# Order of ScalarE's and VectorE's copies around two transposes, and the place of one unit's loads, in an attention kernel with a gated feed-forward layer

## The chip, the cores and the metric

The kernel runs on one core of one Trainium2 chip. The metric is the device time of the whole program in microseconds (us), taken as the median over several runs. The engines are TensorE (PE, with PEld its weight loads), VectorE (DVE), ScalarE (ACT), GpSimd (POOL) and SyncE (SP, which here issues every DMA).

## The reference

Shapes: q, k, v are (4, 8, 576, 64), the feed-forward weights (512, 2048) and (2048, 512), all float32.

```python
scores = scale * np.matmul(q, k.transpose(0, 1, 3, 2))
x = (psi_rel / psi_i)[..., None]            # a position feature of each (i, j)
bias = np.maximum(x @ w1 + b1, 0.0) @ w2    # one value per (i, j) and head
scores = scores + bias.transpose(2, 0, 1)[None]
attn = np.exp(scores - np.max(scores, axis=-1, keepdims=True))
attn = attn / (np.sum(attn, axis=-1, keepdims=True) + 1e-09)
o = np.matmul(attn, v)                      # (B, H, S, D), then (B * S, H * D)
h = o @ w_in
out = (h * np.cos(h)) @ w_out
```

## The kernel before, in words

The program has three stages, and every order in it is written out by hand: each engine takes its instructions in the order in which the code names them.

**Bias stage.** A loop over n = 0 to 36 makes the 36 groups of bias rows. For each, VectorE (line 309) and for some ScalarE (line 311) make four tiles `ht`, TensorE multiplies them (line 325), ScalarE turns the product into `rt` (line 344; the group with index 34 is done by VectorE, line 342), and SP stores `rt` in a scratch tensor `sc` in DRAM (line 345). There are five `rt` buffers, so a sixth `rt` waits until the first one's store has landed. `load_bias` (line 234) reads whole bias tiles `bt` back. Between the groups stand the loads of q and k of the first units, and the transposes of unit 0's k and q.

**Attention stage.** A unit is a pair of heads of one batch entry: 16 units, numbered from 0. Each has five slots, j = 0 to 4, one for each tile of 128 query rows (`tiles = [0, 1, 4, 2, 3]`, where tile 4 holds the last 64 rows of both heads). `slot` writes, for each: the products `s` of q and k (line 413) and VectorE's pass over each head, which adds the bias and takes the minimum of the negated scores (line 426); the exponentials `P` of the slot before (`softmax_exp`, line 446, one call per head); transposes of the normalised `P` of three slots before (line 476), copied out of the PSUM tile `pm` half by ScalarE and half by VectorE (`keep_main`, lines 501 and 504); products with v (`pv`, line 542).

The next but one unit's q and k are also turned here, in two pieces. The left-overs (rows 512 to 575 of k and q, loaded into one tile) are turned in slot 1 into the PSUM tile `pt` (line 196), and `keep_turned(u, "x", ...)` copies k's part twice into `kt` on VectorE (line 211) and q's part twice into `qt` on ScalarE (line 214). The main pieces of q and k are turned in slot 2 into one PSUM tile `spare` (line 476), and `keep_pair` copies q on ScalarE (line 206) and k on VectorE (line 204). The framework lets two engines read one PSUM tile only one after the other, in the order of the code: the engine named second waits for the one named first. `spare` is one of two buffers with the tag `s`, so slot 3's second product needs it free again. For unit 0 all of this stands in slot 2.

`two` is true in slot 2 of units 0 to 13, the slots that turn a main piece.

**Feed-forward stage.** 96 steps of two matrix products each (lines 695 and 750), with the cosine gate between them.

Of the kernel before, what the change touches and what calls it, by code (L numbers as in the profile page):

```python
# [28 lines left out]
def kernel(  # L29
# [11 lines left out]
    nc = tc.nc  # L41
# [71 lines left out]
    with tc.manual_schedule():  # L113
# [19 lines left out]
        kt = st.tile([128, 640], F32, name="kt")  # L133
# [5 lines left out]
        def turned(u, x):  # L139
            return kt if x == "k" else qts[u % 2]  # L140
# [46 lines left out]
        def bank(dt=F32):  # L187
            return ps_t.tile([128, 512], dt, tag="t", name="pt")

        def natural(u, x):  # L190
            return nat[u, "k" if x == "x" else x].rearrange("p r h d -> p r (h d)")

        def turn(u, x, ps):
            n = natural(u, x)
            for i, c in enumerate((4,) if x == "x" else range(4)):
                nc.tensor.transpose(ps[:, 128 * i : 128 * i + 128], n[:, c], ident)
            return ps
# [9 lines left out]

        def keep_turned(u, x, ps):
            if x == "x":
                for at in (0, 576):  # L210
                    nc.vector.tensor_copy(kt[:, at : at + 64], ps[:, 0:64])
                for h in range(2):
                    r = slice(64 * h, 64 * h + 64)
                    nc.scalar.activation(  # L214
                        out=qts[u % 2][r, 512 + 64 * h : 576 + 64 * h], in_=ps[r, 64:128], func=AF.Copy, scale=-0.125
                    )
                return
            o = turned(u, x)[:, 64:576] if x == "k" else turned(u, x)[:, 0:512]
            nc.scalar.activation(
                out=o.rearrange("p (x c) -> p x c", c=4),  # L220
                in_=ps.rearrange("p (c x) -> p x c", c=4),
                func=AF.Copy,
                scale=-0.125 if x == "q" else 1.0,
            )
# [134 lines left out]
        for n in range(len(todo) + 1):  # L359
            now = hts  # L360
            if n < len(todo):
                hts = bias_hid(n + 1) if n + 1 < len(todo) else None
                ps = bias_rows(n, now)
            if held:
                bias_store(*held)
            for t in {19: (0,), 27: (1,), 36: (2, 3)}.get(n, ()):
                load_bias(0, t)
            if n == 11:
                load_bias(0, 4)
            held = (n, ps)  # L370
            if n == 6:
                for x in "kq":
                    load(1, x)
            if n == 16:
                for x in "kq":
                    load(2, x)
            if n in T_FIRST:
                keep_turned(*T_FIRST[n], turn(*T_FIRST[n], bank()))
            if n in S_FIRST:
                for step in S_FIRST[n][1]:  # L380
                    split(0, S_FIRST[n][0], step)
            if n == len(todo):
                abs_w(*wparts[0])
# [58 lines left out]
        def softmax_exp(u, j, h):  # L442
            neg, m = cur.pop((u, j, h))
            if h == 0:
                dn[u, j] = sv.tile([128, 2], F32, tag="dn", name="dn")
            nc.scalar.activation(  # L446
                out=P[u, j][:, 576 * h : 576 * h + 576],
                in_=neg,
                func=AF.Exp,
                bias=m[:, 0:1],  # L450
                scale=-1.0,
                accum_out=dn[u, j][:, h : h + 1],
            )
# [17 lines left out]
        def heads_of(x):  # L471
            return range(2 if tiles[x[1]] < 4 else 1)
# [99 lines left out]
        def slot(i):  # L572
            u, j = divmod(i, 5)
            now, last, prev = get(i), get(i - 1), get(i - 3)
            if now:
                spare = qk(u, j)
            two = now and j == 2 and u + 2 < NU
            for h in heads_of(last) if last else ():
                if h == 1 and two:
                    break  # L580
                softmax_exp(*last, h)
            if prev and prev[1] in (0, 2):
                alloc_half(prev[0], prev[1] // 2)
            first, ahead, behind = [[], []], [], []
            if two:
                for n, x in enumerate("qk"):
                    for c in range(4):
                        at = 256 * n + 64 * c
                        for r in range(2):
                            first[r].append((spare[:, r, at : at + 64], natural(u + 2, x)[:, c]))  # L590
            if prev and j in (2, 4):
                pair_ = [(u - 1, 3), (u - 1, 4)] if j == 2 else [(u, 0), (u, 1)]
                if pair_[0] in P:
                    src = [P[x][:, 512:640] for x in pair_]
                    shared[0] = bank(), src, (pair_[0][0], 0 if j == 4 else 1)
                if pair_[0] in P and (now or j == 4):
                    ahead = [(shared[0][0][:, 128 * n : 128 * n + 64], x) for n, x in enumerate(src)]
            elif j in (0, 3) and shared:
                gone = shared.pop(0)
                behind = [(gone[0][:, 128 * n + 64 : 128 * n + 128], x) for n, x in enumerate(gone[1])]  # L600
            pm = halves(prev, first, ahead, behind)
            if shared and not now and j == 2:
                gone = shared.pop(0)
                for n, x in enumerate(gone[1]):
                    nc.tensor.transpose(gone[0][:, 128 * n : 128 * n + 128], x, ident)
                behind = [gone]
            xt = None
            if i == 0:
                for x in "kq":
                    keep_turned(1, x, turn(1, x, ps_m.tile([128, 512], F32, tag="m0" if x == "k" else "m1", name="pm")))  # L610
                keep_turned(1, "x", turn(1, "x", bank()))
            if now and (j == 1 or i == 2) and i != 1 and u + 2 < NU:
                xt = turn(u + 2, "x", bank())
            for du, hf, chunks in PV_EARLY[j]:
                if 0 <= u + du < NU:
                    pv(u + du, hf, chunks)
            if two:
                keep_pair(u + 2, "q", spare[:, :, 0:256])
                keep_pair(u + 2, "k", spare[:, :, 256:512])
                softmax_exp(*last, 1)  # L620
            if prev:
                keep_main(*prev, 0, pm[0])
            for du, hf, chunks in PV_EARLY[j]:
                if 0 <= u + du < NU and 4 in chunks:
                    keep_x(u + du, hf)
            if prev:
                keep_main(*prev, 1, pm[1])
            if behind:
                keep_left(*gone[2], gone[0][:, 0:256])
            if last:  # L630
                recip(*last, 0)
                recip(*last, 1)
            if now and u == 0 and j == 0:
                split(1, "k")
            elif now and u == 0 and j == 1:
                split(1, "q")
            elif now:
                for du, x, step in POOL_PLAN[j]:
                    if u + du < NU and not (u == 0 and x == "q"):
                        split(u + du, x, step)  # L640
            if xt is not None:
                keep_turned(u + 2, "x", xt)
            if last:
                for h in heads_of(last):
                    norm(*last, h)
            if now:
                if i == 1:
                    load(0, "v")
                for du, x in LOAD_PLAN[j]:
                    if u + du < NU:  # L650
                        load(u + du, x)
                hp, b = units[u]
                if b == B - 1 and hp + 1 < HP:
                    load_bias(hp + 1, tiles[j])
                if u == NU - 1 and j < KD:
                    split_x(0, 0, j)
            for step, at in W_PLAN:
                w, r = divmod(i - 0 - at, 10)
                if r == 0 and 0 <= w < len(wparts):
                    if step == "load":  # L660
                        if w + 2 < len(wparts):
                            load_w(*wparts[w + 2])
                    elif step == "abs":
                        abs_w(*wparts[w])
                    else:
                        widen_w(*wparts[w], step)

        for i in range(len(jobs)):
            slot(i)
# [225 lines left out]
```

## Time and profile before

| | us or share |
|---|---|
| median of 3 runs | 731.68 (731.63 to 733.46) |
| the profiled execution's own time | 731.56 |
| its span | 729.8 |
| PE busy | 96% |
| DVE busy | 82% |
| ACT busy | 60% |
| POOL busy | 55% |

The span is the profiled part of the program, from its first to its last instruction; the execution's own time has a little more around it. A busy share is that of the whole span, over all three stages.

### The profile page before, as it was taken

The numbers are of one execution on the slowest core, as the hardware profiler recorded it, in microseconds if no ns is written. First come the engines' busy times: TensorE is split into PE (matmuls) and PEld (weight loads), VectorE is DVE, ScalarE is ACT, GpSimd is POOL, SyncE is SP. The second block draws the span as 40 slices with busy tenths as digits, with TensorE's granted clock in tenths as the row PEclk, the third lists the DMA queues.
The fourth block names the chain that finished last, engine by engine and source line by source line (L and its number), as shares of the span: only waits on it lengthen the run. The fifth ranks groups of instructions, "written<-read, shape, count | busy, mean of one in ns | idle before, by whom it ended". The sixth has DMA issues, their size and how long they took to land.

```text
span 729.8 us, 16094 instructions
## 1 busy us (share of the span) xinstructions
PE 701.4 (96%) x5960; PEld 569.9 (78%) x5960; DVE 600.5 (82%) x1371; ACT 435.7 (60%) x917; POOL 402.9 (55%) x486
## 2 busy tenths in 40 slices
PE   6888999999999999999999999999999999999997
PEld 4556766666666666768988989988989988989986
DVE  8988888888888888856778789898998999966665
ACT  6778777777867778754565555445454454443342
POOL 0203877877787787774456274564544463663300
PEclk9999999999999999999999999999999999999999
DMA  6688337434623730100011010102011110011112
GB/s 201 215 268 275 72 94 188 120 81 105 171 51 91 198 82 19 47 30 30 29 35 53 29 59 30 58 29 58 31 31 56 30 58 30 1 41 46 45 44 86
DMA packets 84398, 58.66 MB, mean 80 GB/s; under 512 B 62304, under 2 KB 70624, under 8 KB 84320
## 3 DMA queue, kind: packets, MB, share of 16 engines
q1 hardware_dynamic: 84320, 57.63, 27.6%
q8 instruction: 47, 0.77, 0.4%
q14 instruction: 31, 0.25, 0.1%
HBM read 42.00 MB, written 15.61 MB: 79 GB/s over the span
## 4 chain that ended last, share of the span: by engine, by line
PE 84%; DVE 8%; ACT 4%; DMA 2%; issue 2%; POOL 1%; SPq 0%; DVEq 0%; ACTq 0%; POOLq 0%
PE ph L695 28%; PE po L750 27%; PE pv L542 10%; PE s L413 9%; PE pa L325 4%; PE pm L476 4%; DVE P L426 3%; ACT P L446 2%; DVE ht L309 1%; DVE kt L204 1%; DMA sc<-rt 1%; ACT qt L206 1%; DVE PT L504 1%; ACT qt L214 1%; PE pt L476 1%
## 5 line engine op out<-in xcount | busy, mean ns | idle before, releaser
L469 POOL TENSOR_SCALAR P<-P,rc 128x576 f32<-128x576 f32 x144 | 108.2, 763 | 46.0 <-PE s L413 29.0
L426 DVE CUSTOM_DVE_ANT_0 P<-s,bt 128x576 f32<-128x576 f32 x144 | 103.8, 754 | 15.8 <-PE s L413 13.0
L699 ACT ACTIVATE a<-ph,quarter 128x384 int32<-128x384 f32 x96 | 55.7, 581 | 101.2 <-PE ph L695 100.1
L527 POOL TENSOR_TENSOR xs<-xT,xs 128x384 fp32r<-128x384 f32 x96 | 107.1, 1116 | 8.0
L446 ACT ACTIVATE P<-P,m 128x576 f32<-128x576 f32 x144 | 110.3, 769 | 0.7 <-DVE m L426 0.3
L413 PEld LDWEIGHTS s<-kN,qT 64*128 64x128 f32 (+1 forms) x864 | 72.2, 187 | 47.7 <-DVE m L426 14.8
L695 PE MATMUL ph<-xs,wpre 128*128 128x384 f32 x576 | 109.4, 338 | 0.0
L695 PE MATMUL ph<-xs,w 128*128 128x384 f32 x576 | 108.3, 337 | 0.0
L705 DVE SCALAR_TENSOR_TENSOR r<-a,ph 128x384 f32<-128x384 int32 x96 | 52.8, 550 | 67.0 <-ACT a L699 66.8
L695 PEld LDWEIGHTS ph<-xs,wpre 128*128 128x128 f32 x576 | 101.8, 188 | 5.7 <-DVE a L714 0.9
L413 PE MATMUL s<-kN,qT 64*128 64x288 f32 (+1 forms) x864 | 94.7, 314 | 11.9 <-DVE kt L204 10.0
L695 PEld LDWEIGHTS ph<-xs,w 128*128 128x128 f32 x576 | 101.5, 188 | 4.8 <-DVE a L714 0.6
L710 ACT ACTIVATE r<-r,hpi 128x384 f32<-128x384 f32 x96 | 59.3, 617 | 73.8 <-DVE r L706 73.6
L526 POOL TENSOR_SCALAR xs<-xT 128x384 fp32r<-128x384 f32 x96 | 63.4, 660 | 38.9 <-PE ph L695 38.9
L724 DVE TENSOR_TENSOR gl<-a,gh 128x384 fp32r<-128x384 f32 x96 | 74.4, 775 | 2.1 <-ACT gh L718 2.1
L542 PE MATMUL pv<-PT,vN 128*64 128x320 f32 (+1 forms) x512 | 76.0, 418 | 0.0
L750 PE MATMUL po<-wpre,gh 128*128 128x512 f32 x288 | 75.3, 397 | 0.0
L750 PE MATMUL po<-w,gh 128*128 128x512 f32 x288 | 75.2, 395 | 0.0
L111 POOL TENSOR_TENSOR w<-wb,w 128x512 fp32r<-128x512 f32 x16 | 20.8, 1298 | 89.5 <-ACT w L109 89.5
L706 DVE SCALAR_TENSOR_TENSOR r<-a,r 128x384 f32<-128x384 int32 x96 | 61.0, 635 | 3.3
L718 ACT ACTIVATE gh<-a 128x384 fp32r<-128x384 f32 x96 | 49.7, 518 | 21.6 <-DVE a L714 21.6
L476 PE MATMUL pm<-ident,P 64*128 64x64 f32 x1184 | 59.9, 225 | 1.0 <-POOL P L469 1.0
(95 smaller groups left out, 1197.5 us busy)
## 6 DMA issues: line engine op xcount, KB each, us to landing
sc<-rt SPq DMA_DIRECT2D x36, 295.5 KB, 3.5
raw<-in_moe_w_in_dram SPq DMA_DIRECT2D x16, 512.0 KB, 3.7
raw<-in_moe_w_out_dram SPq DMA_DIRECT2D x16, 512.0 KB, 3.6
bt<-sc SPq DMA_DIRECT2D x16, 288.0 KB, 3.3
nk<-in_k_dram SPq DMA_DIRECT2D x32, 128.0 KB, 3.4
nq<-in_q_dram SPq DMA_DIRECT2D x32, 128.0 KB, 3.3
bt<-sc SPq DMA_DIRECT2D x16, 256.0 KB, 3.6
vN<-in_v_dram SPq DMA_DIRECT2D x32, 128.0 KB, 2.7
```

The source lines that it names most:

```text
L413: nc.tensor.matmul(s[h][:, hf, 0:HALF], qTs[u % 2][r, a, 128 * t : 128 * t + 128] if t < 4 else qTs[u % 2][:, a, 512:640], kN[u][r, b, o : ...
L426: nc.vector.tensor_tensor_reduce(neg.rearrange("p (a x) -> p a x", a=2), s[h][:, :, 0:HALF], bias[hp, t, h].rearrange("p (a x) -> p a x", ...
L446: nc.scalar.activation(out=P[u, j][:, 576 * h : 576 * h + 576], in_=neg, func=AF.Exp, bias=m[:, 0:1], scale=-1.0, accum_out=dn[u, j][:, h ...
L469: nc.gpsimd.tensor_scalar(p, p, r, 1.0, ALU.mult, ALU.mult)
L476: nc.tensor.transpose(out, i[p], ident[p, p], tile_position=(64 * r, 0))
L526: nc.gpsimd.tensor_scalar(h, src, 1.0, 1.0, ALU.mult, ALU.mult)
L527: nc.gpsimd.tensor_tensor(l, src, f(h), ALU.subtract)
L542: nc.tensor.matmul(ps[64 * h : 64 * h + 64, 0 : WQ[hf]], a, m, start=(c == 0), stop=(c == 4), tile_position=(r.start, 64 * h), skip_group_ ...
L695: nc.tensor.matmul(ps, a, x, start=(i == 0), stop=(i == 3 * KD - 1))
L706: nc.vector.scalar_tensor_tensor(r, n, -TWO_PI_LO, r, ALU.mult, ALU.add)
L724: nc.vector.tensor_tensor(gl, a, f(G[key][0]), ALU.subtract)
L750: nc.tensor.matmul(O[n][i], a[:, 128 * i : 128 * i + 128], w, start=(i0 == 0 and p == 0), stop=(i0 == GF - 1 and p == 2),)
```

## The change

Three orders are changed. In `keep_turned` for the left-overs, ScalarE's two copies of q stand ahead of VectorE's two copies of k, so that now VectorE is the one that waits. In slot 2, the exponentials of both heads stand ahead of the copy of q out of `spare`; before, the second head's came behind it. In the bias stage, the six loads of k and q of unit 2 stand at n = 35 and no longer at n = 16.

```diff
         def keep_turned(u, x, ps):
             if x == "x":
-                for at in (0, 576):
-                    nc.vector.tensor_copy(kt[:, at : at + 64], ps[:, 0:64])
                 for h in range(2):
                     r = slice(64 * h, 64 * h + 64)
                     nc.scalar.activation(
                         out=qts[u % 2][r, 512 + 64 * h : 576 + 64 * h], in_=ps[r, 64:128], func=AF.Copy, scale=-0.125
                     )
+                for at in (0, 576):
+                    nc.vector.tensor_copy(kt[:, at : at + 64], ps[:, 0:64])
                 return
...
-            if n == 16:
+            if n == 35:
                 for x in "kq":
                     load(2, x)
...
             two = now and j == 2 and u + 2 < NU
-            for h in heads_of(last) if last else ():
-                if h == 1 and two:
-                    break
-                softmax_exp(*last, h)
+            if last:
+                for h in heads_of(last):
+                    softmax_exp(*last, h)
...
             if two:
                 keep_pair(u + 2, "q", spare[:, :, 0:256])
                 keep_pair(u + 2, "k", spare[:, :, 256:512])
-                softmax_exp(*last, 1)
```

ScalarE's rows in a unit's slots 1 to 3, before: the copy of `pm` that ends slot 1, the left-overs `qt<-pt`, the exponentials `P`, the main piece `qt<-spare`. In brackets stand the engines whose semaphores a row waits for.

```order
L501 ACTIVATE PT_2353<-pm 128x8x64 [waits PE_49]
L214 ACTIVATE qt_107<-pt 64x64 [waits DVE_49,PE_49]
L214 ACTIVATE qt_107<-pt 64x64
L446 ACTIVATE P,dn<-P,m 128x576 [waits Pool_49]
L206 ACTIVATE qt_107<-spare 128x512 [waits PE_49]
L446 ACTIVATE P,dn<-P,m 128x576
L501 ACTIVATE PT_2353<-pm 128x8x64 [waits PE_49]
```

The same place with the change.

```order
L501 ACTIVATE PT_2353<-pm 128x8x64 [waits PE_49]
L212 ACTIVATE qt_107<-pt 64x64 [waits PE_49,Pool_49]
L212 ACTIVATE qt_107<-pt 64x64
L446 ACTIVATE P,dn<-P,m 128x576 [waits DVE_49] x2
L206 ACTIVATE qt_107<-spare 128x512 [waits PE_49]
L501 ACTIVATE PT_2353<-pm 128x8x64 [waits PE_49]
```

The left-overs no longer wait for VectorE, and one exponential has moved from behind the main piece to ahead of it.

VectorE at the end of slot 1 and in slot 2, before: copies of `pm`, the sums `dn` and their reciprocals `rc`, the left-overs `kt<-pt`, the pass over tile 4 (`P,m<-s,bt`), the main piece `kt<-spare`.

```order
L504 COPY PT_1386<-pm 128x8x64 [waits PE_49]
L459 TENSOR_SCALAR dn<-dn 128x1 [waits Activation_49] x2
L462 RECIPROCAL rc<-dn 128x2 [waits DVE_49]
L211 COPY kt<-pt 128x64 [waits PE_49]
L211 COPY kt<-pt 128x64 [waits Pool_49]
L426 ISA P,m<-s,bt 128x576 [waits PE_49]
L426 ISA m 128x1
L204 COPY kt<-spare 128x512 [waits Activation_49]
```

The same place with the change.

```order
L504 COPY PT_1386<-pm 128x8x64 [waits PE_49]
L459 TENSOR_SCALAR dn<-dn 128x1 [waits Activation_49] x2
L462 RECIPROCAL rc<-dn 128x2 [waits DVE_49]
L216 COPY kt<-pt 128x64 [waits PE_49,Activation_49]
L216 COPY kt<-pt 128x64 [waits Pool_49]
L426 ISA P,m<-s,bt 128x576 [waits PE_49]
L426 ISA m 128x1
L204 COPY kt<-spare 128x512 [waits Activation_49]
```

Nothing moves on VectorE; the first copy of k's left-overs has a wait for ScalarE that it did not have.

SP's queue in the last part of the bias stage, with the change (before, the rows `nk` and `nq` stood ahead of the third last store to `sc_72`, and the stores to `sc_74` were followed at once by the loads `bt`).

```order
L345 DMA sc_73<-rt 128x591
L345 DMA sc_74<-rt 128x591 x7
L162 DMA nk<-in_k_dram 128x4x64 x2
L165 DMA nk<-in_k_dram 64x2x64
L165 DMA nk<-in_q_dram 64x2x64
L162 DMA nq<-in_q_dram 128x4x64 x2
L345 DMA sc_74<-rt 128x591
L234 DMA bt<-sc_73 128x576
L234 DMA bt<-sc_73 128x64
L234 DMA bt<-sc_73 128x512
L234 DMA bt<-sc_74 128x576
```

The six loads now stand ahead of the last store and of the six loads of the bias tiles 2 and 3.

## Rows read from the trace of the kernel before

**Rows 1.** The page: busy us of each engine, share of the span, instructions.

```profile
PE 701.4 (96%) x5960; PEld 569.9 (78%) x5960; DVE 600.5 (82%) x1371; ACT 435.7 (60%) x917; POOL 402.9 (55%) x486
```

**Rows 2.** Waits: waiter <- releaser: us in all, times, the longest.

```profile
PE s L413 <- DVE kt L204: 10.0, 13, 0.9
```

**Rows 3.** Timeline of unit 7: start us, us, engine, what, [idle before <- releaser].

```profile
175.47 0.33 PE L196 MATMUL pt<-ident,nk 128*128 128x128 f32 x1
175.53 0.59 ACT L501 ACTIVATE PT<-pm 128x512 f32<-128x512 f32 x1
...
176.32 0.75 DVE L426 CUSTOM_DVE_ANT_0 P<-s,bt 128x576 f32<-128x576 f32 x1
...
178.04 0.41 PE L476 MATMUL spare<-ident,nk 64*128 64x64 f32 x8
...
178.35 0.45 ACT L214 ACTIVATE qt<-pt 64x64 f32<-64x64 f32 x2 [2.23 <-DVE kt L211]
...
178.83 0.78 ACT L446 ACTIVATE P<-P,m 128x576 f32<-128x576 f32 x1
...
179.72 0.60 ACT L206 ACTIVATE qt<-spare 128x512 f32<-128x512 f32 x1
...
179.76 0.40 PE L413 MATMUL s<-kN,qT 64*128 64x288 f32 x1
...
180.35 0.69 DVE L204 COPY kt<-spare 128x512 f32<-128x512 f32 x1 [1.42 <-ACT qt L206]
...
181.10 1.06 PE L413 MATMUL s<-kN,qT 64*128 64x288 f32 x11 [0.94 <-DVE kt L204]
```

**Rows 4.** Timeline of unit 6, the same place.

```profile
160.79 0.59 ACT L501 ACTIVATE PT<-pm 128x512 f32<-128x512 f32 x1
...
162.27 0.45 ACT L214 ACTIVATE qt<-pt 64x64 f32<-64x64 f32 x2 [0.89 <-PE s L413]
...
163.64 0.60 ACT L206 ACTIVATE qt<-spare 128x512 f32<-128x512 f32 x1
...
165.02 1.06 PE L413 MATMUL s<-kN,qT 64*128 64x288 f32 x11 [0.57 <-DVE kt L204]
```

**Rows 5.** Timeline of the bias stage (SPq: SP's issue of DMAs).

```profile
27.09 0.36 DVE L211 COPY kt<-pt 128x64 f32<-128x64 f32 x2 [0.76 <-PE pt L196]
...
27.55 0.44 ACT L214 ACTIVATE qt<-pt 64x64 f32<-64x64 f32 x2
...
36.32 1.29 SPq L162 DMA_DIRECT2D nk<-in_k_dram  x2
...
40.95 1.55 SPq L345 DMA_DIRECT2D sc<-rt  x3
...
44.13 0.84 ACT L344 ACTIVATE rt<-pa,cst,mrow 128x591 f32<-128x591 f32 x1 [2.14 <-DMA sc<-rt]
...
46.69 4.18 DVE L309 TENSOR_SCALAR ht<-lt,pk,edge 128x368 f32<-128x368 f32 x10 [0.98 <-PE pa L325]
...
49.80 1.62 ACT L344 ACTIVATE rt<-pa,cst,mrow 128x591 f32<-128x591 f32 x2 [1.65 <-DMA sc<-rt]
...
51.93 9.34 DVE L309 TENSOR_SCALAR ht<-lt,pk,edge 128x416 f32<-128x416 f32 x21 [1.06 <-PE pa L325]
```

**Rows 6.** Timeline of the end of the bias stage and of unit 0.

```profile
62.38 0.32 SPq L345 DMA_DIRECT2D sc<-rt  x1
...
67.99 0.46 PE L476 MATMUL spare<-ident,nq 64*128 64x64 f32 x8
...
70.24 1.06 PE L413 MATMUL s<-kN,qT 64*128 64x288 f32 x11 [0.93 <-DVE dn L459]
...
71.22 0.76 DVE L426 CUSTOM_DVE_ANT_0 P<-s,bt 128x576 f32<-128x576 f32 x1 [0.43 <-PE s L413]
```

**Rows 7.** DMA issues, 36 to 41 us: count, KB each, us to landing.

```profile
nq<-in_q_dram SPq DMA_DIRECT2D x2, 128.0 KB, 3.0
```

**Rows 8.** Stretch 72 to 76: length, busy us of PE, PEld, DVE, ACT, POOL, granted clock, DMA.

```profile
72.00:76.00 4.00, 3.84 (x41) 3.51 (x43) 3.87 (x11) 2.86 (x9) 3.82 (x7) 0.57 0.61 135
```

## The prediction

> **What bounds the kernel now.** I read the page first. TensorE is busy 96% of the span [rows 1], and the chain that ended last runs through it in all of the feed-forward stage, so a microsecond that TensorE gains earlier is a microsecond off the end. Then the waits, for TensorE alone: nearly all of its idle time in the attention stage is one wait, slot 3's product of q and k behind VectorE's copy of k out of `spare`: 10.0 us in 13 pieces, one in each of units 1 to 13 [rows 2]. Then the timeline around each of them. They come in two kinds: seven odd units like unit 7, where TensorE stands idle 0.94 us [rows 3], and six even ones like unit 6, where it is 0.57 us [rows 4]; 7 x 0.94 + 6 x 0.57 = 10.0, the whole sum. (ScalarE also converts feed-forward weights in slot 4 of odd units, and so comes late into the even ones.) Last I read the bias stage and unit 0, which the moved loads touch [rows 5 to 8].
>
> What holds the copy in unit 7, back from the product [rows 3]: TensorE goes on at 181.10, behind VectorE's copy (180.35 to 181.04), which waited 1.42 us for ScalarE's copy of q (179.72 to 180.32). ScalarE had no idle time just ahead of that; its idle time lies further back, 2.23 us ahead of the left-overs at 178.35, which waited for VectorE's copies of k's left-overs. So a wait early in ScalarE's queue is paid at its end by TensorE.
>
> **The change, part by part.** Its sum is made against the profiled execution's own 731.56 us, 0.12 below the median.
>
> *Odd units.* With the left-overs of q first, ScalarE can go on as soon as slot 1's copy is done: 175.53 + 0.59, so about 176.14. TensorE's turn of the left-overs ended at 175.80, so nothing else holds it. The two left-over copies take 0.48 to the next start (178.35 to 178.83). Both exponentials now follow. Their inputs are there (VectorE's second pass ends at 177.07). One takes 0.78 to the next exponential (its duration) and 0.89 to a copy behind it (178.83 to 179.72). That makes 176.14 + 0.48 + 0.78 + 0.89 = 178.29. But the copy of q also needs the turned pieces in `spare`, which end at 178.04 + 0.41 = 178.45; with 0.06 for handing over (as from 181.04 to 181.10) it starts at 178.51. It ends at 179.11, VectorE's copy runs 0.03 later from 179.14 to 179.83, and TensorE goes on at 179.89 in place of 181.10: 1.21 us gained. This is more than the 0.94 of idle time, since the first product of the block stood at 179.76 and ran alone; an unbroken block would gain 1.34, which is the upper bound. The lower is 0.6, if VectorE, after a wait of 1.42 shrinks, becomes the next to hold the block. I take 1.21, as VectorE's own idle time goes by the same amount and it moves ahead with TensorE. Seven units: 8.5 us. VectorE's new wait for ScalarE costs nothing here: ScalarE's left-overs would end near 176.6, and VectorE's copies of k run just ahead of 178.35. Were ScalarE late instead, VectorE's pass over tile 4, queued behind, would wait, and with it the next product.
>
> *Even units.* The same steps [rows 4]: 160.79 + 0.59 and the hand-over give 161.40, + 0.48 + 0.78 + 0.89 = 163.55, against 163.64 now. The freed 0.89 us of idle time is almost all spent on the exponential that now stands first. The gain is 0.09, bounded by -0.02 (0.89 for each exponential) and 0.2 (0.78 for each). Six units: 0.5 us. The exponential that moves is no loss behind the copy: nothing waits for it there before its sum in the same slot.
>
> *Left-overs in the bias stage.* The reordered copies also stand at n = 12. There VectorE copies at 27.09, and ScalarE only at 27.55, behind `rt`, until 27.99 [rows 5]. VectorE now comes second, at 28.02: 0.93 us later. Nothing covers this: from there until the end of the stage VectorE has just two idle pieces, 0.98 and 1.06 us, so it sets the stage's pace. Cost 0.9.
>
> *Loads away from n = 16.* The six loads hold SP from 36.32 to 40.95, 4.63 us, with stores of `rt` behind them; two `rt` then wait 2.14 and 1.65 us for a store to land, and VectorE gets its two idle pieces from that, 2.04 us in all [rows 5]. Without the loads I expect all of it back (bounds 1.0, if the loads of the first bias tiles still crowd the stores, and 2.04). Both together: the stage ends 1.1 us sooner.
>
> *Loads at n = 35.* The store ahead of them leaves at 62.38 [rows 6], then 1.1 sooner, 61.27; with its 0.32 the loads begin at 61.6, and by 4.63 for six end at 66.2. The last issues some 0.77 (a sixth) before that, at 65.45, and lands 3.0 us later [rows 7]: 68.45. It brings half of q of unit 2, which TensorE turns at 67.99 now and could turn at 66.9. So it starts 0.46 later than now, the 1.1 us are used up, and the copies and slot 3's product at 70.24 follow it. Net loss 0.5, bounds -1.1 (data there in time) and 1.5 (landing a microsecond slower). The last store and the bias loads behind the loads are covered: tile 2's would issue by 66.6 and land by about 69.6, and VectorE wants it at 71.22; tile 3's wait for the last store's landing and come a slot's length later, as does their use.
>
> [...]
>
> Sum: 731.56 - 8.5 - 0.5 + 0.5 = **723.1 us**.
>
> **The rivals.** *A new wait takes half.* VectorE is busy 82% [rows 1], and more in this stage; if in odd units the next product waits for it, 0.6 remains of 1.21: 727.4. For it: with the 1.42 gone VectorE works nearly without a break in slots 0 to 3. Against it: its idle time shrinks as TensorE's does. [...] *Slower: the exponential ahead of the copy.* If ScalarE's left-overs start no sooner than now (held by TensorE's turn or by another wait in place of VectorE's), the moved exponential delays the copy by 0.89 in each of 13 units: 731.6 + 11.6 = 743. It decides where less than 0.78 to 0.89 is freed; even units are on that edge, odd ones free 2.2. If the even units alone lose it, 6 x 0.89 = 5.3 us of the gain go: 729. *The change does nothing*: reordered copies hidden behind TensorE's own queue, 731.6; the idle 10.0 us speak against it.
>
> **How the numbers follow.** My forecast, 721 to 725.3, has 0.58; less than that (718.5 to 721, the 1.1 us of the bias stage kept) 0.05; the second fall and late loads 0.12; half the gain 0.13; within 0.3% 0.06; slower 0.06. About 0.3% (2.2 us) is what a measurement of this kernel can tell from no change. So faster has 0.88. The range from 719.8 to 727.5 takes in the forecast, most of the case below it, the second fall and a part of the half gain, some 0.8.
>
> **What would show it.** Right: in odd units ScalarE's left-overs start with slot 1's copy and no longer wait for VectorE, TensorE's wait for the copy of k falls below 0.1 us there, and stays near 0.5 in even ones; in the bias stage no `rt` waits some 2 us for a store; in unit 0 TensorE waits for `nq`. Wrong: a new TensorE wait of about a microsecond per unit for VectorE's `m` or GpSimd's `P`, left-overs that still start late, or a mean clock as low as now over much more than 4 us.

## The result, and the profile after

The change measured **721.52 us** (median of 4 runs, 720.94 to 722.11), against 731.65 us (731.37 to 733.46, 4 runs) for the kernel before beside it: a ratio of 0.9856, 95% interval 0.9838 to 0.9875. That is 1.6 us under the forecast of 723.1, inside the range, and faster by well over 0.3%. The profiled execution took 721.16 us, its span is 719.4 us, against 731.56 and 729.8 before: 10.4 us less by both measures.

The page's first part, after. The answer to [rows 1]: every busy time is within 0.9 us of what it was. No work went away; TensorE's share rises because the span shrank around it.

```profile
span 719.4 us, 16106 instructions
...
PE 700.5 (97%) x5960; PEld 569.3 (79%) x5960; DVE 599.7 (83%) x1371; ACT 435.8 (61%) x917; POOL 403.0 (56%) x486
```

The waits, after, TensorE in the attention stage (60 to 310 us). The answer to [rows 2], where slot 3's product waited 10.0 us in 13 pieces for VectorE's copy of k.

```profile
PE s L413 <- DVE kt L204: 2.5, 7, 0.6
PE s L413 <- DVE m L426: 1.6, 4, 0.9
PE spare L476 <- DVE m L426: 0.8, 1, 0.8
```

Seven pieces are left: 0.32 in each of six even units and 0.60 in unit 0. The seven odd ones are gone. The single new piece of 0.8 is in unit 0 and is read below.

The timeline of unit 7, after, the answer to [rows 3].

```profile
171.10 0.60 ACT L501 ACTIVATE PT<-pm 128x512 f32<-128x512 f32 x1
...
171.59 0.44 ACT L212 ACTIVATE qt<-pt 64x64 f32<-64x64 f32 x2
...
172.06 0.78 ACT L446 ACTIVATE P<-P,m 128x576 f32<-128x576 f32 x1
...
172.83 0.76 ACT L446 ACTIVATE P<-P,m 128x576 f32<-128x576 f32 x1
...
173.62 0.41 PE L476 MATMUL spare<-ident,nk 64*128 64x64 f32 x8
...
174.07 0.60 ACT L206 ACTIVATE qt<-spare 128x512 f32<-128x512 f32 x1 [0.39 <-PE spare L476]
...
174.70 0.69 DVE L204 COPY kt<-spare 128x512 f32<-128x512 f32 x1 [0.18 <-ACT qt L206]
...
175.16 1.35 PE L413 MATMUL s<-kN,qT 64*128 64x288 f32 x12
```

ScalarE's 2.23 us of idle time ahead of the left-overs is gone. Its copy of q now waits for TensorE's transposes (0.39) instead of being late for them: those end at 173.62 + 0.41 = 174.03, and it starts 0.04 later. VectorE's wait falls from 1.42 to 0.18, and the twelve products of slot 3 run as one block, where before one ran and eleven waited.

The timeline of unit 6, after, the answer to [rows 4].

```profile
156.61 0.59 ACT L501 ACTIVATE PT<-pm 128x512 f32<-128x512 f32 x1
...
157.08 0.46 ACT L212 ACTIVATE qt<-pt 64x64 f32<-64x64 f32 x2
...
158.33 0.41 PE L476 MATMUL spare<-ident,nk 64*128 64x64 f32 x8
158.34 0.76 ACT L446 ACTIVATE P<-P,m 128x576 f32<-128x576 f32 x1
...
159.22 0.60 ACT L206 ACTIVATE qt<-spare 128x512 f32<-128x512 f32 x1
...
160.59 1.06 PE L413 MATMUL s<-kN,qT 64*128 64x288 f32 x11 [0.32 <-DVE kt L204]
```

Here the transposes are done at 158.74, and ScalarE is still in the second exponential until it starts the copy at 159.22. So ScalarE, not TensorE, sets the copy's start: 0.48 us late, of which TensorE's unfinished block hides all but 0.32.

The timeline of the bias stage, after, the answer to [rows 5] and to the first row of [rows 6].

```profile
27.23 0.44 ACT L212 ACTIVATE qt<-pt 64x64 f32<-64x64 f32 x2
...
27.70 0.36 DVE L216 COPY kt<-pt 128x64 f32<-128x64 f32 x2 [1.69 <-ACT qt L212]
...
60.24 0.32 SPq L345 DMA_DIRECT2D sc<-rt  x1
...
60.64 1.06 PE L413 MATMUL s<-kN,qT 64*128 64x288 f32 x12
60.65 1.30 SPq L162 DMA_DIRECT2D nk<-in_k_dram  x2
```

VectorE's wait at 27.70 is 0.93 longer than the 0.76 before. After it, no `rt` waits for a store any more, and VectorE works from 27.97 to the stage's end without an idle piece. The first product of the attention stage starts at 60.64, against 62.50 before: 1.86 us sooner. Of this, 0.32 is not the change's: at n = 12, ahead of the first changed instruction, VectorE is free for its copies at 27.70 - 1.69 = 26.01, and before at 27.09 - 0.76 = 26.33. From there to the first product it is 34.63 us in place of 36.17, so 1.54 less.

The timeline of unit 0, after, the answer to the rest of [rows 6], and below it a row of windows (columns as in [rows 8]).

```profile
63.38 1.24 SPq L162 DMA_DIRECT2D nq<-in_q_dram  x2
...
67.19 0.69 PE L476 MATMUL spare<-ident,nq 64*128 64x64 f32 x8 [0.83 <-DVE m L426]
...
69.84 1.80 PE L413 MATMUL s<-kN,qT 64*128 64x288 f32 x11 [0.60 <-DVE kt L204]
```

```profile
64.00:80.00 16.00, 13.04 (x147) 10.56 (x145) 12.29 (x45) 11.35 (x31) 13.96 (x19) 0.79 0.72 188
```

TensorE turns q of unit 2 at 67.19, 0.80 sooner than before, although the stage's first product came 1.86 sooner; counted from that product the turn is 1.06 later (6.55 us behind it, before 5.49). The granted clock is 0.50 from 67.0, just ahead of that turn, to 73.9 us (by windows of 0.5 us: 0.53 in the first, 0.64 in the last, 0.50 in each between); inside that stretch eleven products take 1.80 us where they took 1.06 before, at a granted 1.00. The mean over 64 to 80 is 0.79, so 16 x 0.21 = 3.4 us of clock are lost. Before, the same 16 us have 0.89, a loss of 1.8, in one stretch of half that length, from 72.3 to 75.7, most of it in [rows 8]: 4 x (1 - 0.57) = 1.7. What clock is lost is not yet time lost, since TensorE waits in part of the stretch (0.60 ahead of 69.84).

**Where the 10.4 us came from**, by the starts of unit 0's first product and of ScalarE's copy of q (line 206) in units 1 and 13, in us of the profiled executions:

| stretch | before | after | difference |
|---|---|---|---|
| start to first product of unit 0 | 62.50 | 60.64 | -1.86 |
| from there to unit 1's copy | 21.58 | 22.19 | +0.61 |
| unit 1's copy to unit 13's | 191.66 | 182.44 | -9.22 |
| the rest | 454.1 | 454.1 | about 0 |

The second stretch holds the gain of one odd unit, some 1.2, so unit 0 itself lost 1.8. Of these, 1.06 lie ahead of the turn of q. In the third, an even unit's copy to the next odd one's takes 14.84 in place of 16.06, an odd one's to the next even one's 15.56 in place of 15.81.

### The profile page after: what moved, and what is told of

It is laid out like the page before. It is cut to its first block, busy times and chain, and to the rows that moved or that the text cites. A ratio compares the mean times of both kernels' runs of the same rounds, so it can differ in the third digit from the quotient of the medians.

```text
span 719.4 us, 16106 instructions
## 1 busy us (share of the span) xinstructions
PE 700.5 (97%) x5960; PEld 569.3 (79%) x5960; DVE 599.7 (83%) x1371; ACT 435.8 (61%) x917; POOL 403.0 (56%) x486
## 4 chain that ended last, share of the span: by engine, by line
PE 87%; DVE 6%; ACT 2%; issue 2%; DMA 1%; POOL 0%; SPq 0%; DVEq 0%; ACTq 0%
PE ph L693 28%; PE po L748 28%; PE pv L542 10%; PE s L413 9%; PE pa L325 5%; PE pm L476 4%; DVE P L426 2%; ACT P L446 1%; DVE ht L309 1%; DVE PT L504 1%; PE pt L476 1%; PE spare L476 1%; DVE kt L204 1%; DMA lt<-in_ltab_dram 1%; ACT qt L206 1%
## 5 line engine op out<-in xcount | busy, mean ns | idle before, releaser
L708 ACT ACTIVATE r<-r,hpi 128x384 f32<-128x384 f32 x96 | 59.3, 617 | 73.6 <-DVE r L704 73.4
L501 ACT ACTIVATE PT<-pm 128x512 f32<-128x512 f32 (+1 forms) x80 | 43.9, 549 | 34.7 <-PE pm L476 31.4
```

The lines of the kernel that those rows point to most:

```text
L708: nc.scalar.activation(out=r, in_=r, func=AF.Sin, scale=SIN_SCALE, bias=hpi)
```

## The experiments

The theory: the gain is that of the left-overs' order, which lets ScalarE begin early; the exponential ahead of the copy is at best free; the moved loads help the bias stage and hurt unit 0. The rivals: the exponentials are what fills TensorE's gap; the loads are worth nothing. Ratios are to the kernel before beside each set: 732.3 (731.29 to 733.55) for the first four kernels and 732.34 (731.22 to 734.45) for the last four, 9 runs each. Beside the change it was 731.65, so a difference in us between the change and a kernel of these sets can be off by some 0.7; by ratios such differences are given where they matter.

### The left-overs alone

The kernel before, with this piece of the change:

```diff
             if x == "x":
-                for at in (0, 576):
-                    nc.vector.tensor_copy(kt[:, at : at + 64], ps[:, 0:64])
                 for h in range(2):
...
+                for at in (0, 576):
+                    nc.vector.tensor_copy(kt[:, at : at + 64], ps[:, 0:64])
                 return
```

> Only q's left-overs ahead of k's; the second head's exponential stays behind the copy of q, the loads of unit 2 stay at n = 16. Theory (the gain is ScalarE's freed wait, and the moved exponential only spends some of it again): odd units gain the whole 1.3 us as with the change, even units more than with it, since the copy of q can start at the end of the transposes, 0.66 us sooner than before, against 0.25 with the change; 7 x 1.3 + 6 x 0.66 = 13.1 us, unit 0 and the bias stage as before or up to 0.9 later: 718.5 to 719.5, and TensorE waits for the copy of k in no unit for more than 0.3 us. Rival (the moved exponential is itself worth something, since the sums and reciprocals behind it come sooner): 721.5 or above.

Measured: 721.96 us (720.15 to 723.18), ratio 0.985 (0.9832 to 0.9868). So this edit alone gives what all three together give. The waits of TensorE, 60 to 310 us, in this kernel: none for the copy of k is left.

```profile
PE pm L476 <- POOL P L469: 1.6, 3, 0.7
PE s L413 <- DVE m L426: 1.3, 3, 0.9
PE s L413 <- DVE dn L459: 0.9, 1, 0.9
```

The timeline of its unit 6: one exponential, then the copy, which now waits for the transposes in the even units too.

```profile
158.28 0.78 ACT L446 ACTIVATE P<-P,m 128x576 f32<-128x576 f32 x1
...
159.52 0.60 ACT L206 ACTIVATE qt<-spare 128x512 f32<-128x512 f32 x1 [0.38 <-PE spare L476]
160.01 0.77 ACT L446 ACTIVATE P<-P,m 128x576 f32<-128x576 f32 x1
```

Unit 1's copy to unit 13's is 179.86, 11.8 us less than before and 2.6 less than with the whole change. So the lengths of the units are those of the theory, while the median is 2.5 us above the theory's upper end. The later first product (63.42, 0.92 later than before) does not explain that, since the theory had counted up to 0.9 for it. The profiled execution took 720.15, the fastest of this kernel, and is 0.65 above the theory; there the stretch from the first product to unit 1's copy takes 21.02, 0.66 more than the 21.58 of before less the 1.22 that an odd unit gains. The other three took 721.79 to 723.18. The first two of them have the mean clock of the profiled one (0.995 and 0.996, against 0.995), so a lower mean clock is not what made them longer, and the rest stays open. Two rows of unit 1's first slot, for comparison with a later kernel:

```profile
76.79 0.48 PE L413 MATMUL s<-kN,qT 64*128 64x288 f32 x1
...
78.88 1.08 PE L542 MATMUL pv<-PT,vN 128*64 128x256 f32 x8
```

### The exponentials alone

The kernel before, with this piece of the change:

```diff
-                if h == 1 and two:
-                    break
                 softmax_exp(*last, h)
...
-                softmax_exp(*last, 1)
```

> Only both exponentials ahead of the copy of q; left-overs and loads as before. Theory (the exponential is paid by the copy wherever nothing has been freed for it): 13 units lose 0.75 to 0.9 us each, 741.5 to 743. Rival (ScalarE has room, the order there is hidden): 731.6.

Measured: 751.18 us (746.92 to 755.52), ratio 1.0251 (1.0198 to 1.0304), slower by more than expected. The timeline of its unit 7, the wait that stands for the whole attention stage, and two windows:

```profile
185.49 0.45 ACT L214 ACTIVATE qt<-pt 64x64 f32<-64x64 f32 x2 [2.23 <-DVE kt L211]
...
187.62 0.60 ACT L206 ACTIVATE qt<-spare 128x512 f32<-128x512 f32 x1
...
188.99 1.06 PE L413 MATMUL s<-kN,qT 64*128 64x288 f32 x11 [1.69 <-DVE kt L204]
```

```profile
PE s L413 <- DVE kt L204: 20.7, 14, 1.7
```

```profile
120.00:160.00 40.00, 36.28 (x443) 26.02 (x445) 31.40 (x102) 27.58 (x71) 29.98 (x40) 0.96 0.44 107
200.00:240.00 40.00, 36.15 (x440) 25.68 (x439) 29.01 (x101) 27.89 (x73) 29.03 (x38) 0.96 0.33 79
```

ScalarE still idles 2.23 us behind VectorE's k, and the second exponential now adds its length to that: the wait for the copy of k grows from 10.0 to 20.7 us. These 10.7 us are near the 11.6 that the prediction's slower rival counts. The rest goes with a lower clock: the mean over the span is 0.988 of 745.1 us, 8.9 us lost, where before 0.996 of 729.8 is 2.9. Two stretches of 40 us in the middle of the stage are granted 0.96, and the 20 us from 280 on 0.91, which before happens in none; unit 0's low stretch has 0.79 over 64 to 80 us, 3.4 us lost. The two slowest runs, 754.0 and 755.52, have a mean clock of 0.978 and 0.977, so some 8 us more of clock lost than in the profiled one at 746.92, and about as much time. Where in those runs the clock was low is not known.

### The loads alone

The kernel before, with this piece of the change:

```diff
-            if n == 16:
+            if n == 35:
```

> Only the loads of unit 2 at n = 35. Theory (the bias stage gains what its stores no longer wait for, 2.0 us, and unit 0 gives it back by late data and a second fall of the granted clock, 1.7): 731 to 732, the first product of the attention stage some 2 us sooner, the clock low over some 7 us in place of 3.5. Rival (the loads are part of the gain, and the second fall seen with the whole change was chance): 729.5.

Measured: 730.4 us (730.05 to 731.48), ratio 0.9973 (0.9962 to 0.9985): a gain of 1.9. The theory stood for a gain of at most 0.6 against the 731.56 of before, the rival for 2.1, so the rival's size held. The profiled execution took 731.48, the slowest of the six; the other five took 730.05 to 730.47. Its timeline at n = 12 and in unit 0, and the window of 64 to 80:

```profile
26.94 0.36 DVE L211 COPY kt<-pt 128x64 f32<-128x64 f32 x2 [0.76 <-PE pt L196]
...
66.38 0.46 PE L476 MATMUL spare<-ident,nq 64*128 64x64 f32 x8 [0.95 <-DMA nq<-in_q_dram]
```

```profile
64.00:80.00 16.00, 13.58 (x129) 11.34 (x131) 11.27 (x41) 10.88 (x30) 13.21 (x18) 0.68 0.74 193
```

The first product came at 59.88, 2.62 us sooner, and 2.47 sooner counted from VectorE's free moment at n = 12 (33.70 us in place of 36.17). Then TensorE waited 0.95 for q's data, and 16 x 0.32 = 5.1 us of clock were lost in place of 1.8; unit 1's copy came 0.2 later than before. So in this execution the wait for data and the low clock took together what the bias stage gained (1.0 us up to the copy of q in unit 0, 1.84 from there to unit 1's). The fastest of the others, 730.05, has a mean clock of 0.998, against 0.991 here, which is some 5 us of clock for 1.4 us of time. The row also bears on the label in the change's own trace, where the same 0.83 is put down to VectorE's `m`: here the same instruction waits as long and the wait is put down to the load. Nor do these transposes depend on the `m` of the product just ahead of them: before, they started at 67.99 [rows 6], and that `m` came only at 68.78. The `m` ahead of that one, whose pass frees the buffer of `spare`, was done at 65.92 with the change, before the wait began at 66.36.

### Left-overs and exponentials, without the loads

The change, with the loads put back:

```diff
-            if n == 35:
+            if n == 16:
```

> Left-overs and exponentials as in the change, the loads of unit 2 back at n = 16. Theory (loads worth nothing in sum): 721.5, within 0.7. Rival (the moved loads bring the bias stage's 2 us for good): 723.3 or above. In the bias stage VectorE, 0.9 later at n = 12, should lose its two idle pieces of 1 us each instead of ending later, if they are set by the stores alone.

Measured: 724.6 us (723.11 to 725.36), ratio 0.9885 (0.9867 to 0.9903). The rival held: within the change the moved loads are worth 724.6 - 721.5 = 3.1 us, or 2.1 by the two ratios (0.9885 against 0.9856). The waits of this kernel in the bias stage (27 to 62 us):

```profile
ACT rt L344 <- DMA sc<-rt: 4.1, 2, 2.3
...
DVE ht L309 <- PE pa L325: 2.4, 2, 1.2
```

They are those of [rows 5], a little longer (2.14 + 1.65 and 0.98 + 1.06 there), so they don't absorb what VectorE lost to the left-overs; the first product came at 63.57. Two rows of unit 1's first slot:

```profile
76.97 0.40 PE L413 MATMUL s<-kN,qT 64*128 64x288 f32 x1 [1.00 <-DVE m L426]
...
79.74 1.97 PE L542 MATMUL pv<-PT,vN 128*64 128x256 f32 x8
```

From the first product to unit 1's copy this kernel takes 22.57, longer than the change's 22.19, although no data come late here. The mean of its granted clock is 0.77 over 76 to 80 and 0.80 over 80 to 84, 1.7 us of clock lost, as with the left-overs alone (0.70 over 72 to 76, 0.87 over 76 to 80). By my estimate, which takes the 0.50 that the short windows of before and of the change show, these are stretches from 78.2 to 81.6 and from 73.6 to 77.0. But there the low stretch lay where TensorE here waits 1.00 for VectorE's `m`, and here it lies behind that wait, where TensorE has work: eight products with v take 1.97 us in place of 1.08. So in these two executions unit 0's time, 22.57 here and 21.02 there, goes with the place of the low stretch, and that the moved loads cost the change time in unit 0, beyond their wait, is not shown.

### Left-overs and loads, without the exponentials

The change, with the exponentials put back:

```diff
-            if last:
-                for h in heads_of(last):
-                    softmax_exp(*last, h)
+            for h in heads_of(last) if last else ():
+                if h == 1 and two:
+                    break
+                softmax_exp(*last, h)
...
+                softmax_exp(*last, 1)
```

> The whole change without the moved exponentials: left-overs of q first, loads at n = 35. Theory (the moved exponential costs the even units 6 x 0.4 = 2.5 us whatever the loads do, as left-overs alone against left-overs and exponentials showed, 2.6): 719.0, 2.5 below the change; TensorE waits for the copy of k in no unit from 1 to 13. Rival (what the two kernels without moved loads showed was the granted clock): 721.5.

Measured: 718.98 us (718.19 to 720.08), ratio 0.9814 (0.9793 to 0.9834), as expected, 2.5 us under the change (3.1 by the ratios). Unit 1's copy to unit 13's is 179.85, as with the left-overs alone. So the exponentials are a loss of 2.6 us in these units, inside a change that wins. TensorE waits for the copy of k in no unit.

### The exponentials in odd units only

The kernel with the left-overs alone, and in it:

```diff
-                if h == 1 and two:
+                if h == 1 and two and u % 2 == 0:
                     break
...
-                softmax_exp(*last, 1)
+                if u % 2 == 0:
+                    softmax_exp(*last, 1)
```

> Left-overs of q first, both exponentials ahead of the copy of q in odd units only, loads at n = 16. Theory (in odd units the copy of q waits for the transposes, so the moved exponential is hidden; only even units pay): 722.0, as with the left-overs alone. Rival (odd units pay too): 723.3 or above, halfway to the 724.6 of left-overs and exponentials.

Measured: 720.91 us (720.49 to 721.78), ratio 0.984 (0.9821 to 0.986). Unit 1's copy to unit 13's is 179.81: in odd units the second exponential lies wholly under the wait for the transposes, and the loss of 2.6 is that of six even units, 0.44 each.

### k first in units 0 and 1, with the loads late

The kernel with left-overs and loads, and in it:

```diff
             if x == "x":
+                if u < 2:
+                    for at in (0, 576):
+                        nc.vector.tensor_copy(kt[:, at : at + 64], ps[:, 0:64])
                 for h in range(2):
...
-                for at in (0, 576):
-                    nc.vector.tensor_copy(kt[:, at : at + 64], ps[:, 0:64])
+                if u >= 2:
+                    for at in (0, 576):
+                        nc.vector.tensor_copy(kt[:, at : at + 64], ps[:, 0:64])
```

> As the run before, but the left-overs of units 0 and 1 (bias stage and slot 0) keep k's copies first. Theory (the new order costs VectorE 0.9 us at n = 12 with nothing to cover it): the attention stage's first product some 0.8 us sooner, but the data of unit 2 come with the last stores, so that at least half of it stays: 718.0 to 718.7. Rival (those 0.9 us are idle time that the stage has anyway): no difference, 719.0.

Measured: 718.9 us (717.1 to 719.11), ratio 0.9801 (0.978 to 0.9822): no clear difference from 718.98. The timeline of its unit 0 and the window:

```profile
66.30 0.46 PE L480 MATMUL spare<-ident,nq 64*128 64x64 f32 x8 [1.14 <-DVE m L430]
```

```profile
64.00:80.00 16.00, 13.65 (x141) 11.60 (x141) 11.23 (x42) 10.50 (x28) 13.01 (x18) 0.68 0.73 189
```

The first product came at 59.60, 1.1 sooner, but `spare` then waited 1.14, by the reading above for its data, and the clock's mean over 64 to 80 was 0.68. In this execution unit 0 took 0.5 us longer (23.56 from the first product to unit 1's copy, against 23.06), half of what the bias stage gave. The five runs fall in two groups: three of 718.9 to 719.1 with a mean clock of 0.992 or 0.993, the profiled one among them, and two of 717.1 and 717.3 with 0.997.

### The same, with the loads split

The kernel just above, and in it:

```diff
-            if n == 35:
-                for x in "kq":
-                    load(2, x)
+            if n == 23:
+                load(2, "k")
+            if n == 31:
+                load(2, "q")
```

> As the run before, but unit 2's k loads stand at n = 23 and its q loads at n = 31, so that neither lies with the first bias tiles' loads nor ahead of the last store. Theory (unit 0 waits for late data and TensorE's clock falls twice): unit 0's transposes wait for no data, the clock falls once, 1.7 us less; if the four loads at n = 23 cost stores no more than 0.5 us, 716.5 to 717.3. Rival (the loads hold up stores wherever they stand in the stage): the bias stage longer by 1 to 2 us, 718 to 719.

Measured: **716.81 us** (715.7 to 717.28), ratio 0.9781 (0.9761 to 0.98), as expected and the fastest kernel here, 4.7 us under the change. Its timeline of the bias stage and unit 0, and the window:

```profile
53.42 0.84 ACT L348 ACTIVATE rt<-pa,cst,mrow 128x591 f32<-128x591 f32 x1 [1.81 <-DMA sc<-rt]
...
65.77 0.46 PE L481 MATMUL spare<-ident,nq 64*128 64x64 f32 x8
```

```profile
64.00:80.00 16.00, 12.82 (x161) 9.80 (x162) 14.48 (x49) 12.91 (x35) 15.41 (x22) 1.00 0.66 166
```

One `rt` still waits 1.81 for a store, and the first product comes at 60.33, 0.73 later than with the loads at n = 35. But q is there when TensorE wants it, and in this execution, 716.37, the granted clock is 1.00 from 60 to 84 us and 0.999 over the span. Two of the four runs have that mean, 715.7 and 716.37; 717.25 and 717.28 have 0.996 and 0.995. These last two are no faster than the two faster runs of the kernel just above. From the first product to unit 1's copy it takes 20.27, against 23.56 in the kernel just above, 22.19 in the change and 21.58 before.

## Why the prediction was right, and where its terms were off

**Odd units: right.** Forecast 1.21 us for each of seven; measured 16.06 - 14.84 = 1.22. The chain of reasons is in the trace too: the left-overs start with slot 1's copy, the copy of q starts on the transposes' end, the block runs unbroken. The first rival (VectorE takes half) fell: TensorE's wait for `m` is 1.6 us in 4 pieces in the whole stage.

**Even units: the mechanism right, the term mis-sized.** Forecast 0.09 for each of six, bound 0.2; measured 15.81 - 15.56 = 0.25, and the same from TensorE's wait, 0.57 to 0.32. The chain of two exponentials and the copy came as priced (0.78 + 0.88). The step that was off is the one ahead of it: I let the left-overs start when slot 1's copy had ended and been handed over, 0.61 after its start; in the trace they start 0.47 after it (156.61 to 157.08), 0.12 before the copy's 0.59 us are over. Six times 0.16 is 1.0 us. The stretch from unit 8 to 9, one of the odd units' gains, gained a further 0.4, since it took 16.42 before; with the loads alone, whose code there is the same, it took 16.06, so this is no effect of the change.

**The exponential: priced, and not set against leaving it alone.** The forecast says that behind the copy the exponential is no loss, and that is right: the kernels that leave it there are the faster ones. It also says that the freed time is almost all spent on it in even units. What it lacks is the conclusion that the even units would gain more without it: beside the same kernel with the exponential left behind the copy, the change loses 2.6 us in units 1 to 13, and alone the edit cost more than the slower rival's 11.6. The sum did not need this step, as 0.48 + 0.78 + 0.89 held the price.

**Bias stage: one term right, one mis-sized.** Counted from VectorE's free moment at n = 12 to the first product, the stage takes 36.17 us before, 34.63 with the change, 33.70 with the loads alone, 34.64 with left-overs and loads, and 33.70 with k first in units 0 and 1 and the loads late. So beside late loads the left-overs cost 0.93 or 0.94, as forecast, and the loads away from n = 16 gave 2.47, not 2.04: VectorE's two idle pieces were not all that they cost. What the other 0.4 us were was not tested; two executions with the same code here differ by 0.2 (36.17, and 35.95 with the exponentials alone). With the loads at n = 16 the left-overs cost 0.9 to 1.3 (37.04 to 37.44 in three kernels). Together 1.54 in place of 1.1; the further 0.32 of the 1.86 was there ahead of the change.

**Unit 0: two errors that nearly cancel, by luck.** q of unit 2 was turned at 67.19, not 68.45, since the loads began at 60.65 and not at 61.6, and took 3.97 us and not 4.63. So counted from the first product the turn came 1.06 later than before, 0.83 of it TensorE's wait, where I had 1.57. But I counted nothing for the clock, and its low stretch lasted 6.8 us in place of 3.4; the other 0.8 of the 1.8 lost came with it. A mean clock as low as before (0.57 over 72 to 76, [rows 8]) over much more than 4 us was one of the prediction's own signs of being wrong, and it came: 0.51 over 67 to 74. This was the case of late loads and a second fall of the clock, which has a chance of 0.12, in part: the data were less late than forecast, and 3.4 - 1.8 = 1.6 us more of clock were lost, at about half of that in time. No run shows by itself what a fall of the clock costs in time, nor what brings it on, so the chance and the part of the range given to a second fall rest on my estimate alone. What the runs show is how much clock went: 3.4 us where `spare` waits 0.83 (the change) and 0.90 (left-overs and loads), 5.1 where it waits 0.95 (the loads alone) and 1.14 (k first); without such a wait 1.7 in four kernels (before among them), none with the loads split, and 3.4 with the exponentials alone.

**The sum.** Forecast -8.5 - 0.5 + 0.5 = -8.5. Measured: seven odd units -8.5, six even ones -1.5, the wider one -0.4, bias stage and unit 0 together about 0 (-1.86 + 1.8): -10.4. So the even units and the bias stage each gave more, and unit 0 took the bias stage's part back. That unit 0 took so much is a fact of these two executions: the change without the moved loads lost as much there, with its clock low at another place.

**What stays open.** Why the clock fell in or behind unit 0, with a wait for `nq` and without one, why its low stretch falls where it does, and why it did not fall there in the profiled execution with the loads split, although other short waits of TensorE stand there too (0.74, 0.93 and 0.91). The mean clock of each run accounts for part of the spread between runs (the exponentials alone; k first with the loads late), and not for that of the left-overs alone. There a low stretch of the same length at a worse place is a candidate, not shown: unit 0 takes 21.02 us from the first product to unit 1's copy with the left-overs alone and 22.52 with the exponentials moved in odd units, with 1.7 us of clock lost in both.

## What to carry to other kernels

Where two engines read one shared tile in the order of the code, consider naming first the one whose queue has a long tail that something waits for, and look for the idle piece far back in that queue, not at the wait that it ends in. Put work ahead of a critical copy only where the copy would be waiting anyhow: the same exponential was free in odd units (the copy waited 0.39 us for TensorE) and cost 0.44 us in even ones; and time each edit of a bundle alone, since here one edit gave the gain and another took 2.6 us of it. A load is better placed neither ahead of stores that somebody waits for (2.14 and 1.65 us here) nor just ahead of its use (0.95 with the loads alone); here the loads in two pieces and earlier beat the same loads late in one (716.8 against 718.9, with runs of the two that touch).

## What the runs showed of the hardware that was not expected

TensorE's granted clock fell in an attention stage where its idle pieces are at most 1.7 us long: with the exponentials alone (20.7 us in 14 pieces behind the copy of k) two stretches of 40 us were granted 0.96. Inside the low stretches of unit 0 windows of 1 us have 0.50 (73 to 75 before, 68 to 73 with the change, 68 to 78 with k first). In and behind unit 0 the clock lost was 1.7 us before and in three kernels with the loads at n = 16, 3.4 with the change, with left-overs and loads and with the exponentials alone, 5.1 with the loads alone and with k first, and none in the profiled execution with the loads split.

Clock lost was not the same as time lost. The six runs with the loads alone have mean clocks of 0.991 to 0.998, 5 us of clock apart, and are 1.4 us apart. With the left-overs alone and with the change less its loads the same 1.7 us of clock fell at different places, once where TensorE would have waited 1.00 for VectorE and once where it had work.

Rows of ScalarE overlap in places: two copies of 0.60 and 0.59 us had the next activation begin 0.49 and 0.47 behind their start (171.10 to 171.59, 156.61 to 157.08), while the copy behind an exponential of 0.76 us began 0.88 behind that one's start (158.34 to 159.22), with a row of 0.19 between them (ACTIVATION_READ_ACCUMULATOR, at 159.01).
